# A planner that keeps engines apart on a PSUM bank and counts GpSimd and TensorE with other costs

## The chip, the cores and the metric

The kernel runs on one core of one Trainium2 chip. The metric is device time in microseconds, from several timed runs of the same program; the profile shows one execution of it, taken by the hardware profiler. TensorE (PE) multiplies and transposes, VectorE (DVE) and ScalarE (ACT) work on elements, GpSimd (POOL) takes some of DVE's work, and SyncE (SP) issues DMAs. PE alone writes PSUM here; DVE and ACT read it.

## The reference

Pooled attention for 4 batches of 8 heads, and then a low-rank mix over the tokens and an MLP, all in float32:

```python
q_pool = q.reshape(B, H, S // 2, 2, D).mean(axis=3)      # 4 x 8 x 576 x 64
scores = scale * np.matmul(q_pool, k.transpose(0, 1, 3, 2))   # S = 1152 keys
attn = np.exp(scores - max); attn = attn / (sum + 1e-9)
x = (attn @ v), heads joined                             # 4 x 576 x 512
u = x + ((x.T @ U) @ V).T                                # rank 32
out = u + np.maximum(u @ w_ch1, 0) @ w_ch2               # 512 -> 2048 -> 512
```

## The kernel before

**What is computed where.** Each of the 32 heads is one call of `head(n)`. The keys and queries of a head are turned by PE (L538 for queries, L616 for the keys of batches 0 and 1, L571 for those of batches 2 and 3), and the turned blocks are taken out of PSUM by ACT and DVE. In batches 2 and 3 this is `turn_whole`: ACT reads the bank in L580, L587, L591 and L595, DVE reads the same bank in L582. A scan finds row maxima: 14 products of 384 or 288 key columns on PE (L643, L645), each reduced by DVE (L649). Then 14 score products (L703 and L704, 256 to 640 columns in a bank) whose exponentials ACT writes to `big` (L710). DVE or POOL add up the exponentials into `acc` (L686). The values are 36 MATMUL instructions a head (L735), and the sums of a pair of heads are L726, L772, L759.

After the 8 heads of a batch comes `tail(b)`. First the low-rank mix: x times U (L818), a copy to SBUF by ACT (L824, L825), two DMAs that lay the copy beside itself (L827, issued by SP), an ACT copy (L828) and a DVE difference (L830), then that times V (L837) and five DVE additions into X (L839). Then X is turned (L909) and split by ACT and DVE (L918, L919). Then the MLP: 24 products for a block of the hidden layer (L943) or, in the last batch, a form with fewer products (L987), and the way back (L1058, L1062). The MLP of batch b runs among the heads of batch b+1. In the first batch the float64 weights are decoded (L415 to L427, L867, L868) by ACT, DVE and POOL.

**What sets the order.** No order is written by hand. Every piece of work is an `op` with a due number, the engines that can run it, a cost in nanoseconds for each, and the keys that it reads and writes. `Plan.run` is a greedy planner: it keeps a clock for each engine, and gives each the earliest-due op that can start at once or within 30 ns (`SLACK`) of the first. An op can start when its inputs are there (their planned end plus a latency from the table `LAT`), its engine is free and a buffer is free. Ops that DVE or POOL can run (`dual`: L514, L528, L686, L868, L962, L967) go to the one that would end first, with a bias of 300 ns for DVE; L551 goes to ACT or POOL. The planner's order is only the order in which each engine's instructions stand in the program. The waits are semaphores that the tile layer adds by itself. PSUM has 8 banks, 5 of them in pool `m` and 3 in pool `s`.

**Names that the change touches.** `Slot` is one buffer, a PSUM bank for `m` and `s`. `pick` chooses the next op of an engine; its last loop makes an op wait for the former users of a buffer (`b.wait`). `g_(n)` is the planned cost of n columns on POOL, `mm(n)` of n columns on PE, `TSW` what a group of value products costs beside its columns, `TP` and `TPR` what a transpose costs, `FILL` what one of the 70 filler transposes (L479) costs, which keep PE busy when it has nothing else to do early on.

Of the kernel before, what the change touches and what calls it, by code (L numbers as in the profile page):

```python
# [32 lines left out]

class Slot:
    def __init__(self, tile_):
        self.tile, self.user = tile_, None


class Op:
# [3 lines left out]
class Plan:  # L43
# [46 lines left out]
    def run(self, slack, bias, bias_from, link):  # L90

        lat = self.LAT
        for o in self.ops:
            o.open = len(o.deps)
            for d in o.deps:
                d.succ.append(o)
        free = dict.fromkeys(lat, 0.0)
        free["pool"] = 4000.0
        port = wire = 0.0
        cand = {e: [] for e in lat}  # L100
        key = lambda o: (o.at, o.seq)

        def offer(o):
            for e in o.ways:
                base = max([d.end + lat[d.way][e] for d in o.deps], default=0.0)
                cand[e].append((o.at, o.seq, base, o))
                cand[e].sort()

        def slot_of(b, e, taken=()):
            best = None  # L110
            if b.line and b.line[0] is not b:
                return None
            if b.keep and sum(s.user is None or not s.user.left for s in b.slots) <= b.keep:
                return None
            for s in b.slots:
                u = s.user
                if s in taken:
                    continue
                if u is None:
                    return 0.0, s  # L120
                if u.left == 0:
                    t = max(x.end + lat[x.way][e] for x in u.done)
                    if best is None or t < best[0]:
                        best = (t, s)
            return best

        def late(o, e, t):

            shift = bias if t > bias_from else 0.0
            for c in o.ways:  # L130
                if c != e:
                    end = free[c]
                    for at, seq, base, x in cand[c]:
                        if x is o:
                            if max(end, base) + o.ways[c][0] + (shift if c == "dve" else -shift) < t + o.ways[e][0]:
                                return True
                            break
                        if base <= end:
                            end += x.ways[c][0]
            return False  # L140

        def pick(e):

            found, first = [], None
            for at, seq, base, o in cand[e][:self.WINDOW]:
                t = max(base, free[e])
                if e == "pool" or (e == "dve" and o.port):
                    t = max(t, port)
                if e == "sp" and len(o.ways[e]) > 4:
                    t = max(t, wire - 1100)  # L150
                if first is not None and t > first + slack:
                    continue
                taken = []
                for b in o.bufs:
                    if b.slot is None:
                        got = slot_of(b, e, taken)
                        if got is None:
                            t = None
                            break
                        t = max(t, got[0])  # L160
                        taken.append(got[1])
                    else:
                        for x in b.wait:
                            t = max(t, x.end + lat[x.way][e])
                if t is None or (len(o.ways) > 1 and late(o, e, t)):
                    continue
                found.append((t, o))
                if first is None or t < first:
                    first = t
                if t <= free[e]:  # L170
                    break
            for t, o in found:
                if t <= first + slack:
                    return t, o
            return None

        for o in self.ops:
            if not o.open:
                offer(o)
        order, choice = [], dict.fromkeys(lat)  # L180
        while len(order) < len(self.ops):
            for e in lat:
                choice[e] = pick(e)
            e = min((c for c in lat if choice[c]), key=lambda c: choice[c][0])
            t, o = choice[e]
            for b in o.bufs:
                if b.slot is None:
                    b.slot = slot_of(b, e)[1]
                    if b.line:
                        b.line.popleft()  # L190
                    b.wait = b.slot.user.done if b.slot.user else ()
                    b.slot.user = b
                b.left -= 1
                b.done.append(o)
            cost = o.ways[e][0]
            o.way, o.start = e, t
            if e == "sp":
                hold, far = (*o.ways[e][2:], 0, 0, 0)[:2]
                issue = 475 + hold
                free[e] = t + issue + 25  # L200
                wire = max(wire, t + issue + 625) + cost
                o.end = wire + far
            else:
                free[e] = o.end = t + cost
                if len(o.ways[e]) > 2:
                    o.end += o.ways[e][2]
                if e == "pool" or (e == "dve" and o.port):
                    port = o.end
            for c in o.ways:
                cand[c] = [x for x in cand[c] if x[3] is not o]  # L210
            for x in o.succ:
                x.open -= 1
                if not x.open:
                    offer(x)
            order.append(o)
        self.order = order
        turn = None
        for o in order:
            ins = o.ways[o.way][1]()
            if o.way == "dve" and o.port:  # L220
                turn = ins
            elif o.way == "pool" and turn is not None:
                link(ins, turn)
                turn = None
# [3 lines left out]
def kernel(  # L228
# [25 lines left out]
    NJ = S // P  # L254
    HALF = NQ // 2
# [6 lines left out]
    QT, KS = -9.86, -11.64  # L262
# [2 lines left out]
    NB, QUICK = 320, (False, False, False, True)  # L265
    NARROW, NP2 = 256, 7
    GV = [((0, 6), (6, 9))] + [((0, 9),)] * 3
    TSW = 300.0
    SUM, AV, YT = 0.71, 0.51, 0.79
    NS = 6  # L270
    LOOSE = (1, 0, 0, 0)
    APART = (True, True, False, False)
    KT, MX0, MXS = 0.79, -8.77, 4.16
    V_LO = slice(2 * R, 3 * R)
    WARM_UP, WARM_N, FILL, FILL_N = 5000.0, 13, 90.0, 70
    NWHOLE = H + 1
    EXP_MIN, EXP_MAX = 2.0 ** -15, 122879.9921875
    SCALE = 0.5 / float(D) ** 0.5
# [13 lines left out]
    op = plan.op  # L292
    sb = ctx.enter_context(tc.tile_pool(name="sb", bufs=1))
    dram = ctx.enter_context(tc.tile_pool(name="dram", bufs=1, space=bass.MemoryType.DRAM))
    ps = ctx.enter_context(tc.tile_pool(name="ps", bufs=1, space=PSUM))

    def slots(name, n, shape, dtype=F32, pool=sb):
        return [Slot(pool.tile(shape, dtype, name=f"{name}{i}")) for i in range(n)]

    ident = sb.tile([P, P], F32, name="ident")  # L300
    identr = sb.tile([P, P], F32R, name="identr")
# [8 lines left out]
    def cut(of, first, n, shape, rows=P):  # L310
# [13 lines left out]
        qp=slots("qp", 1, [QP, NQT, D]),  # L324
        T1=cut(room, 0, 2, (S,)),
        T2=cut(room, 2 * S, 2, (S,), D + 1),
        Q1=cut(room, 5 * S, 2, (NQ,)),
        Q2=cut(room, 6 * S, 2, (PAD + NQ,), D + 1),
# [44 lines left out]
        return 0.52 * n + 67  # L373

    def g_(n):
        return 2.127 * n + 137

    def mm(n):
        return n / 2.4 + 13.0

    def copies(n, first, f, hold=0):

# [5 lines left out]
    def dual(n, f):  # L388
        return {"dve": (v_(n), lambda: f(nc.vector)), "pool": (g_(n), lambda: f(nc.gpsimd))}

    TP, TPR, MOVE = 109, 84, 130
    RATE, BULK = 330.0, True

    def dma(nbytes):
# [104 lines left out]
    def head(n):  # L499
        op = plan.op if n < len(heads) - 4 else lambda at, ways, r=(), w=(), port=False: plan.op(at, ways, [*r, *arena], w, port)  # L500
        b, h = heads[n]
        par = b % 2
        T = lambda G: begin(n) + G * (SLOT if n >= NWHOLE else SLOT * HEAD0 / HEAD)
# [33 lines left out]
                src = qp.t[:, 2 * t:2 * t + 2].rearrange("p a d -> p (a d)")  # L537
                nc.tensor.transpose(pt.t[:, t * QP:(t + 1) * QP], src, ident[0:QP, 0:QP])  # L538

        op(T(QT), ("pe", 240, qT), [qp, (Q1, "use"), (Q2, "use")], [pt])  # L540

        for e in range(2):
            rows, cs_ = slice(e * D, (e + 1) * D), slice(e * HALF, (e + 1) * HALF)
# [185 lines left out]
        for j0, j1 in GV[b]:  # L729
            last = j1 == NJ and odd and not APART[b]  # L730

            def value(js=range(j0, j1), last=last):
                for j in js:
                    for hf in range(2):
                        nc.tensor.matmul(pa.t[hf * D:(hf + 1) * D, 0:HALF], vt.t[:, j], pu[j].t[:, j % 2, hf * HALF:(hf + 1) * HALF],  # L735
                                         start=(j == 0), stop=(j == NJ - 1))
                if last:
                    total()

            n_ = j1 - j0 + last * parts  # L740
            op(T(j1 - 0.5 + AV), ("pe", n_ * 4 * (HALF / 2.4 + 2.0) + TSW, value),
               [(vt, 0)] + keys(range(j0, j1)) + (summed if last else []), [pa] + ([pk] if last else []))
        op(T(NJ + AV), ("act", a_(HALF, True), lambda: nc.scalar.activation(ay.t[:, odd], pa.t[:, 0:HALF], AF.Copy)), [pa], [(ay, odd)])

        if not odd:
            return
        if APART[b]:
            op(T(NJ + AV), ("pe", parts * 4 * (HALF / 2.4 + 2.0) + TSW, total), summed, [pk])
        op(T(NJ + AV), ("act", a_(HALF, True), lambda: nc.scalar.activation(sr.t, pk.t[:, 0:HALF], AF.Copy)), [pk], [sr])

        first = (0, P, HALF - P)
# [383 lines left out]
```

## Time and profile before

| | |
|---|---|
| median of 3 runs | 894.67 us (892.97 to 895.92) |
| span of the profiled execution | 891.4 us |
| granted TensorE clock | 1.000 of full speed |
| PE busy | 882.0 us |
| DVE busy | 742.6 us |
| ACT busy | 524.9 us |
| POOL busy | 220.3 us |

The profiled execution's span, from the first to the last instruction, is 3.3 us below the median of the timed runs, which hold some time around it. A busy share counts a MATMUL from its start to its modelled end. Two MATMULs overlap in the pipeline, so the next one can start some 0.15 us late, and the engine still counts as busy. Waits on PE are therefore read from the starts in the timeline: the distance from one start to the next.

### The profile page before, as it was taken

The numbers are of one execution on the slowest core, as the hardware profiler recorded it, in microseconds if no ns is written. First come the engines' busy times: TensorE is split into PE (matmuls) and PEld (weight loads), VectorE is DVE, ScalarE is ACT, GpSimd is POOL, SyncE is SP. The second block draws the span as 40 slices with busy tenths as digits, with TensorE's granted clock in tenths as the row PEclk, the third lists the DMA queues.
The fourth block names the chain that finished last, engine by engine and source line by source line (L and its number), as shares of the span: only waits on it lengthen the run. The fifth ranks groups of instructions, "written<-read, shape, count | busy, mean of one in ns | idle before, by whom it ended". The sixth has DMA issues, their size and how long they took to land.

```text
span 891.4 us, 15633 instructions
## 1 busy us (share of the span) xinstructions
PE 882.0 (99%) x5597; PEld 723.0 (81%) x5597; DVE 742.6 (83%) x1481; ACT 524.9 (59%) x1184; POOL 220.3 (25%) x223
## 2 busy tenths in 40 slices
PE   9999999999999999999999999999999999999998
PEld 8787777788787877798887887888878778899987
DVE  8999999889999899788888888787776564898885
ACT  6788888758787787565565657555663331322221
POOL 3334444344544635430001012200200000001110
PEclk9999999999999999999999999999999999999999
DMA  6244564346666564543242332422232255555422
GB/s 172 76 131 139 153 197 125 75 156 198 216 208 217 158 224 144 174 143 87 77 135 69 108 111 70 135 88 88 97 120 83 95 172 189 173 204 187 168 100 102
DMA packets 63635, 124.00 MB, mean 139 GB/s; under 512 B 5931, under 2 KB 33350, under 8 KB 63558
## 3 DMA queue, kind: packets, MB, share of 16 engines
q1 hardware_dynamic: 62214, 118.46, 41.0%
q10 hardware_dynamic: 1344, 4.56, 2.3%
q8 instruction: 44, 0.72, 0.4%
q14 instruction: 33, 0.27, 0.1%
HBM read 96.17 MB, written 21.50 MB: 132 GB/s over the span
## 4 chain that ended last, share of the span: by engine, by line
PE 61%; DVE 6%; ACT 1%; issue 1%; DMA 0%; DVEq 0%; ACTq 0%
PE m L1058 19%; PE m L943 11%; PE m L735 8%; PE s L987 6%; PE s L704 4%; PE s L703 4%; PE m L643 4%; DVE mp L649 1%; PE m L571 1%; DVE acc L686 1%; PE m L909 1%; PE m L759 1%; PE m L818 1%; PE m L726 1%; DVE w L868 0%
## 5 line engine op out<-in xcount | busy, mean ns | idle before, releaser
L710 ACT ACTIVATE big<-s 128x320 f32<-128x320 f32 (+2 forms) x448 | 204.2, 480 | 120.9 <-PE s L704 116.2
L649 DVE TENSOR_REDUCE mp<-m 128x1 f32<-128x384 f32 (+1 forms) x448 | 216.4, 532 | 21.9 <-PE m L643 20.4
L1058 PE MATMUL m<-w,hh 128*128 128x512 f32 x798 | 227.0, 397 | 0.0
L943 PE MATMUL m<-rest,w 128*128 128x512 f32 (+1 forms) x768 | 184.6, 354 | 0.0
L703 PE MATMUL s<-room 128*128 128x256 f32 (+2 forms) x576 | 169.1, 304 | 1.3 <-ACT big L710 0.9
L1058 PEld LDWEIGHTS m<-w,hh 128*128 128x128 f32 x798 | 144.2, 188 | 26.2 <-issue 3.1
L704 PE MATMUL s<-room 65*128 65x256 f32 (+2 forms) x576 | 165.1, 298 | 0.0
L735 PE MATMUL m<-big,v 128*64 128x288 f32 x1152 | 148.5, 410 | 0.0
L943 PEld LDWEIGHTS m<-rest,w 128*128 128x128 f32 x768 | 132.4, 188 | 15.3 <-issue 2.2
L686 POOL TENSOR_TENSOR acc<-acc,big 128x576 f32<-128x576 f32 x66 | 94.2, 1427 | 150.2 <-ACT big L710 68.6
L686 DVE TENSOR_TENSOR acc<-acc,big 128x576 f32<-128x576 f32 x150 | 120.4, 803 | 13.1 <-ACT big L710 10.2
L643 PE MATMUL m<-room 128*128 128x384 f32 x384 | 128.4, 358 | 0.5 <-DVE mp L649 0.3
L735 PEld LDWEIGHTS m<-big,v 128*64 128x64 f32 x1152 | 79.2, 137 | 55.5 <-issue 2.0
L703 PEld LDWEIGHTS s<-room 128*128 128x128 f32 x576 | 109.0, 189 | 13.9 <-issue 4.4
L704 PEld LDWEIGHTS s<-room 65*128 65x128 f32 x576 | 108.9, 189 | 6.0 <-DMA room<-mr 0.2
L643 PEld LDWEIGHTS m<-room 128*128 128x128 f32 x384 | 69.6, 189 | 17.6 <-DVE mp L649 3.1
L383 ACT ACTIVATE room<-m 64x288 fp32r<-64x288 f32 (+1 forms) x173 | 72.3, 427 | 9.0 <-PE m L538 6.4
L1062 DVE TENSOR_TENSOR X<-m,X 128x512 f32<-128x512 f32 x95 | 64.7, 683 | 11.0 <-PE m L1058 10.6
L427 POOL TENSOR_TENSOR wt<-wt,rx 128x512 int32<-128x512 int32 (+2 forms) x35 | 44.4, 1269 | 80.8 <-DVE wt L425 19.1
L551 POOL CAST qb<-room 64x64 fp32r<-64x64 f32 x56 | 15.8, 283 | 171.8 <-DVE acc L686 114.2
L947 ACT ACTIVATE hh<-m 128x512 fp32r<-128x512 f32 (+1 forms) x64 | 33.0, 515 | 32.3 <-PE m L943 29.6
L949 DVE SCALAR_TENSOR_TENSOR hh<-m,hh 128x512 fp32r<-128x512 f32 (+1 forms) x64 | 37.4, 584 | 16.2 <-ACT hh L947 15.9
(134 smaller groups left out, 1064.7 us busy)
## 6 DMA issues: line engine op xcount, KB each, us to landing
w<-wc SPq DMA_DIRECT2D x96, 512.0 KB
rx<-in_moe_w_ch_dram SPq DMA_DIRECT2D x32, 512.0 KB
wc<-w SPq DMA_DIRECT2D x32, 512.0 KB
q<-in_q_dram SPq DMA_DIRECT2D x32, 288.0 KB
v<-in_v_dram SPq DMA_DIRECT2D x32, 288.0 KB
k<-in_k_dram SPq DMA_DIRECT2D x31, 288.0 KB
room<-room ACTq DMA_DIRECT2D x15, 288.0 KB
out_dram<-X SPq DMA_DIRECT2D x11, 256.0 KB
```

What stands on the lines that cost most here:

```text
L383: ways = {"act": (a_(n, True) + hold, lambda: f(lambda o, i: nc.scalar.activation(o, i, AF.Copy)))}
L643: nc.tensor.matmul(pm.t[:, 0:w], Q1.t[:, t * P - 64:t * P + 64], T1.t[:, cs_], start=True, stop=True)
L649: op(T(MX0 + 0.3 + MXS * u / 14), ("dve", v_(w), lambda c=c, t=t, w=w, pm=pm: nc.vector.reduce_max(mp.t[:, c * 5 + t:c * 5 + t + 1], pm.t[ ...
L686: op(at, dual(NQ, lambda e: e.tensor_tensor(acc.t, a(), b_(), op=ALU.add)), r, [acc])
L703: nc.tensor.matmul(o, T1.t[:, kc], Q1.t[:, qa:qz], start=True, stop=False)
L704: nc.tensor.matmul(o, T2.t[:, kc], Q2.t[:, PAD + qa:PAD + qz], start=False, stop=True)
L710: op(T(when + 0.1), ("act", a_(len(js) * nq, True), lambda js=js, qa=qa, qz=qz, nq=nq, ss=ss, p=pu[j], e=js[0] % 2: nc.scalar.activation(p ...
L735: nc.tensor.matmul(pa.t[hf * D:(hf + 1) * D, 0:HALF], vt.t[:, j], pu[j].t[:, j % 2, hf * HALF:(hf + 1) * HALF], start=(j == 0), stop=(j == ...
L943: op(now, ("pe", mm(nb), lambda c=c, i=i, a=a, bb=bb, w=w, ph=ph, sl=sl: nc.tensor.matmul(ph.t[:, 0:nb], w.t[:, a, c * P:(c + 1) * P], (ul ...
L987: nc.tensor.matmul(bank.t[:, 0:NB], left(a, c), ub.t[:, i, bb, c], start=(c == 0 and j == 0), stop=(c == 1 and j == 2))
L1058: op(now, ("pe", mm(512), lambda f=f, i=i, a=a, bb=bb, w=w, h_=h_: nc.tensor.matmul(po.t, h_.t[:, a, ns], w.t[:, bb], start=(f == fg and i ...
L1062: op(now, ("dve", v_(512), lambda: nc.vector.tensor_tensor(x(), po.t, x(), op=ALU.add)), [po], bk[t])
```

## The change

Each PSUM slot gets a table `seen`: for each engine the last op planned on the bank, by whichever buffer held it. In `pick`, an op on a bank is planned no sooner than the last op of every other engine on this bank has ended, plus the latency from `LAT`. Before, two engines that read one bank could be planned at the same time. The loops of the kernel, the arithmetic and the number of buffers stay as they are, and so do `LAT`, `BIAS`, the due numbers and the choice between engines.

The costs that change: a POOL op by 140 ns more; a PE product of n columns 0.4427 n + 5.5 ns for n / 2.4 + 13 (512 columns 232 for 226, 256 columns 119 for 120); 9 blocks of values 4,521 ns for 4,692; the sums of a pair of heads get 130 ns instead of `TSW`; transposes 89 and 86 ns for 109 and 84; a filler 82 for 90.

```diff
 class Slot:
     def __init__(self, tile_):
-        self.tile, self.user = tile_, None
+        self.tile, self.user, self.seen = tile_, None, None
...
                     else:
                         for x in b.wait:
                             t = max(t, x.end + lat[x.way][e])
+                        for c, x in (b.slot.seen or {}).items():
+                            if c != e:
+                                t = max(t, x.end + lat[c][e])
...
+            for b in o.bufs:
+                if b.slot.seen is not None:
+                    b.slot.seen[e] = o
...
-    TSW = 300.0
+    TSW, TOT = 165.0, 130.0
...
-    WARM_UP, WARM_N, FILL, FILL_N = 5000.0, 13, 90.0, 70
+    WARM_UP, WARM_N, FILL, FILL_N = 5000.0, 13, 82.0, 70
...
     def g_(n):
-        return 2.127 * n + 137
+        return 2.127 * n + 277
     def mm(n):
-        return n / 2.4 + 13.0
+        return 0.4427 * n + 5.5
...
-    TP, TPR, MOVE = 109, 84, 130
+    TP, TPR, MOVE = 89, 86, 130
...
-            op(T(j1 - 0.5 + AV), ("pe", n_ * 4 * (HALF / 2.4 + 2.0) + TSW, value),
+            op(T(j1 - 0.5 + AV), ("pe", n_ * 4 * (HALF / 2.4 + 1.0) + TSW + last * TOT, value),
```

The instructions of PE are the same 4,943 in both programs, in another order. The order changes on all engines, nearly from the start. POOL has 219 for 228 instructions that belong to the work: 6 fewer L514, 4 fewer L551, 2 fewer L686, 1 fewer L868, and 2 more L528, 1 more L962, 1 more L967. What POOL gives up, DVE has, and in the case of L551 ACT. The lines of the changed kernel are numbered 9 higher from L475 on, so that L837 is L846 there.

The first place is PE behind the low-rank mix of batch 0. L837 (L846 after) adds the mix, L909 (L918) turns X for the MLP, L703 and L704 (L712 and L713) are scores of the next head; `m_` and `s_` are PSUM banks. Before:

```order
L837 MATMUL m_120<-xs_111,Vst 128x512
L837 MATMUL m_121<-xs_111,Vst 128x512
L837 MATMUL m_123<-xs_111,Vst 128x512
L837 MATMUL m_119<-xs_111,Vst 128x512
L837 MATMUL m_122<-xs_111,Vst 64x512
L703 MATMUL s_118<-room 128x320
L704 MATMUL s_118<-room 128x320
L909 MATMUL m_120<-ident,X_98 128x128 x4
L909 MATMUL m_121<-ident,X_98 128x128 x4
L703 MATMUL s_117<-room 128x320
L704 MATMUL s_117<-room 128x320
L909 MATMUL m_123<-ident,X_98 128x128 x4
```

On PE at the same place in the changed program:

```order
L846 MATMUL m_123<-xs_111,Vst 128x512
L712 MATMUL s_118<-room 128x288
L713 MATMUL s_118<-room 128x288
L846 MATMUL m_119<-xs_111,Vst 128x512
L846 MATMUL m_122<-xs_111,Vst 128x512
L846 MATMUL m_123<-xs_111,Vst 128x512
L846 MATMUL m_119<-xs_111,Vst 64x512
L918 MATMUL m_122<-ident,X_98 128x128 x4
L918 MATMUL m_123<-ident,X_98 128x128 x4
L918 MATMUL m_119<-ident,X_98 128x128 x4
L918 MATMUL m_122<-ident,X_98 128x128 x4
L735 MATMUL m_123<-acc_82,ones 32x288
```

The scores that stood between the turns of X now stand ahead of the mix, and the mix goes round three banks for five.

The second place is ACT at the start of batch 2, where a head's keys are taken out of one bank (`m_122` before, `m_119` after) into `room` by L580, L591 and L587 (L589, L600 and L596 after). DVE reads the same bank in L582 (L591 after, on DVE). Before:

```order
L580 ACTIVATE room<-m_122 64x4x128
L867 ACTIVATE w_2_109<-wt_102 128x512
L580 ACTIVATE room<-m_122 64x4x128
L591 ACTIVATE room<-m_122 128x512
L710 ACTIVATE big<-s_116 128x320
L419 ACTIVATE wt_103<-rx 128x512
L420 ACTIVATE rx<-rx 128x512
L587 ACTIVATE room<-m_122 64x4x128 x2
```

On ACT at the same place in the changed program:

```order
L589 ACTIVATE room<-m_119 64x4x128 x2
L600 ACTIVATE room<-m_119 128x512
L562 ACTIVATE qb_80<-room 64x64
L596 ACTIVATE room<-m_119 64x4x128 x2
L428 ACTIVATE wt_102<-rx 128x512
L429 ACTIVATE rx<-rx 128x512
L822 ACTIVATE xs_111<-X_99 128x512
```

ACT's five reads of the bank now stand close together, and on DVE other work has come between the two reads of this bank, which stood side by side.

## Rows read from the trace of the kernel before

**Rows 1.** The page: span, and busy time of each engine.
```profile
span 891.4 us, 15633 instructions
PE 882.0 (99%) x5597; PEld 723.0 (81%) x5597; DVE 742.6 (83%) x1481; ACT 524.9 (59%) x1184; POOL 220.3 (25%) x223
```
**Rows 2.** Busy time by stretch: PE, PEld, DVE, ACT, POOL (instructions), clock, DMA.
```profile
0.00:180.00 180.00, 175.08 (x1300) 137.99 (x1300) 166.98 (x360) 146.21 (x336) 71.99 (x83) 1.00 0.47 133
180.00:360.00 180.00, 179.17 (x1091) 142.55 (x1090) 170.25 (x332) 136.01 (x296) 85.07 (x69) 1.00 0.59 194
```
**Rows 3.** PE's timeline: start, length, instruction [idle before <-releaser].
```profile
155.25 0.34 PE L643 MATMUL m<-room 128*128 128x384 f32 x1
155.43 0.31 PE L703 MATMUL s<-room 128*128 128x320 f32 x1
...
155.72 0.34 PE L643 MATMUL m<-room 128*128 128x384 f32 x1
156.27 0.39 PE L703 MATMUL s<-room 128*128 128x256 f32 x1 [0.21 <-ACT big L710]
```
**Rows 4.** Waits of PE's weight loads, 20 to 180 us: total us, times, longest.
```profile
PEld s L703 <- ACT big L710: 3.4, 9, 0.6
PEld m L643 <- ACT big L710: 1.9, 4, 0.5
PEld m L643 <- DVE mp L649: 1.1, 3, 0.6
```
**Rows 5.** Waits over the whole span: who waited for whom.
```profile
DVE room L582 <- ACT room L591: 11.8, 15, 1.3
ACT room L587 <- DVE room L582: 9.5, 13, 0.8
```
**Rows 6.** Waits of PE's weight loads, 360 to 720 us.
```profile
PEld m L759 <- ACT room L587: 0.5, 2, 0.2
```
**Rows 7.** Groups by line on POOL and DVE: busy us, mean ns, idle before.
```profile
L686 POOL TENSOR_TENSOR acc<-acc,big 128x576 f32<-128x576 f32 x66 | 94.2, 1427 | 150.2 <-ACT big L710 68.6 <-DVE mp L649 38.8 <-DVE acc L686 24.5
L514 DVE TENSOR_TENSOR qp<-q 96x384 f32<-96x384 f32 x15 | 8.7, 580 | 1.7 <-DMA q<-in_q_dram 1.6
L686 DVE TENSOR_TENSOR acc<-acc,big 128x576 f32<-128x576 f32 x150 | 120.4, 803 | 13.1 <-ACT big L710 10.2 <-DVE acc L686 0.5
```
**Rows 8.** PE's part of the chain that ended last: start us, us, what.
```profile
740.02 5.51 PE m L943 x24
```
**Rows 9.** Timelines of PE and DVE at the low-rank mix of batch 0.
```profile
161.93 0.45 PE L818 MATMUL m<-xs,U 128*64 128x512 f32 x1
...
169.56 1.43 PE L837 MATMUL m<-xs,Vst 128*128 128x512 f32 x5 [1.18 <-DVE xs L830]
170.82 0.31 PE L703 MATMUL s<-room 128*128 128x320 f32 x1
...
171.12 1.04 PE L909 MATMUL m<-ident,X 128*128 128x128 f32 x8
171.91 0.40 PE L703 MATMUL s<-room 128*128 128x320 f32 x1
...
175.79 6.43 PE L943 MATMUL m<-rest,w 128*128 128x512 f32 x27
...
170.12 2.48 DVE L839 TENSOR_TENSOR X<-m,X 128x512 f32<-128x512 f32 x4
...
173.12 2.47 DVE L919 TENSOR_TENSOR rest<-m,rest 128x512 fp32r<-128x512 f32 x4
```
**Rows 10.** PE's timeline at the mix of batch 1 and of batch 3.
```profile
358.23 0.39 PE L818 MATMUL m<-xs,U 128*64 128x512 f32 x1
...
365.39 1.43 PE L837 MATMUL m<-xs,Vst 128*128 128x512 f32 x5
...
724.60 0.39 PE L818 MATMUL m<-xs,U 128*64 128x512 f32 x1
...
731.07 0.50 PE L837 MATMUL m<-xs,Vst 128*128 128x512 f32 x1 [0.32 <-DVE xs L830]
```

More of the change, by code (lines that the diff above doesn't have):

```diff
@@ L297, in slots @@
     def slots(name, n, shape, dtype=F32, pool=sb):
-        return [Slot(pool.tile(shape, dtype, name=f"{name}{i}")) for i in range(n)]
+        made = [Slot(pool.tile(shape, dtype, name=f"{name}{i}")) for i in range(n)]
+        for x in made if pool is ps else ():
+            x.seen = {}
+        return made
     ident = sb.tile([P, P], F32, name="ident")
@@ L538, in qT @@
                 nc.tensor.transpose(pt.t[:, t * QP:(t + 1) * QP], src, ident[0:QP, 0:QP])
-        op(T(QT), ("pe", 240, qT), [qp, (Q1, "use"), (Q2, "use")], [pt])
+        op(T(QT), ("pe", 194, qT), [qp, (Q1, "use"), (Q2, "use")], [pt])
         for e in range(2):
@@ L747, in head @@
         if APART[b]:
-            op(T(NJ + AV), ("pe", parts * 4 * (HALF / 2.4 + 2.0) + TSW, total), summed, [pk])
+            op(T(NJ + AV), ("pe", parts * 4 * (HALF / 2.4 + 1.0) + TOT, total), summed, [pk])
         op(T(NJ + AV), ("act", a_(HALF, True), lambda: nc.scalar.activation(sr.t, pk.t[:, 0:HALF], AF.Copy)), [pk], [sr])
```

## The prediction

> **What bounds the kernel now.** I read the page first. PE is busy for 882.0 of a span of 891.4 us [rows 1], so the time is PE's work and whatever PE waits. The change adds and removes no PE instruction. It can only change the waits.
>
> Next came the table by stretch [rows 2]. In the first 360 us DVE is busy for 166.98 and 170.25 us of 180 each, that is 93 and 95 per cent, and POOL for less than half. PE shows 4.9 us of idle time in the first stretch, 0.8 in the second. So DVE is the second bound of the first two batches, and that is where PE waits.
>
> Then the timeline of PE, because its busy share hides waits [rows 3]. L643 at 155.25 is followed by the next start 0.18 us later. The same instruction at 155.72 is followed by one at 156.27, 0.55 us later: PE waited 0.37 us, of which the row shows 0.21, for the exponentials of L710. Waits of this kind are many and small. Between 20 and 180 us PE's weight loads waited 3.4 and 1.9 us for L710 and 1.1 us for the maxima of L649 [rows 4], 6.4 us together.
>
> I read the low-rank mix last, since it is a chain that PE must sit out if it has nothing else to do: L818, two copies on ACT, two DMAs, ACT, DVE, L837. From the start of the last L818 to the start of L837 it took 7.63 us in batch 0 (161.93 to 169.56) [rows 9], 7.16 us in batch 1 and 6.47 us in batch 3 [rows 10].
>
> **The change part by part.** All sums are made against the span of 891.4 us; the median of the timed runs is 3.3 us above it.
>
> *PE's own work:* nothing. The instructions are the same, and a planned cost is not a duration.
>
> *The bank rule.* In batches 2 and 3 ACT and DVE take turns on the turned keys. DVE's L582 sat idle 11.8 us for ACT's L591 and ACT's L587 9.5 us for L582 [rows 5], some 0.75 us each time. So the program already holds the two apart, and the old planner did not know it. The new order puts ACT's reads together and other work between DVE's, which takes much of this idle time away. But it is idle time of ACT and DVE. Of PE's waits in these batches only 0.5 us is put down to L587 [rows 6], because DVE has room there and PE has other heads' work. I count a gain between nothing and 2.5 us, which is five times that row, for what comes late behind it without being named; I take 1.0, nearer to the row.
>
> ACT L587's 9.5 us are 13 waits of 0.73 us on a bank of which the two engines read different halves of the partitions, for the first L587 and the second L582 at least [rows 5]. The Trainium skill (PSUM — Partial Sum Buffer, "PSUM bank collisions raise a hardware error") asks for a guard by bank and 32-partition quadrant only, and calls the whole bank the simple version; by that, the planner now keeps apart what might overlap. If the two did overlap, the new rule would give away up to these 9.5 us of ACT's time, and PE nothing like it. The row says that the program waits in either case, so by the row the rule costs nothing, and I go by the row.
>
> *The costs of POOL.* An addition of 576 columns on POOL took 1,427 ns [rows 7]; the old plan said 1,362, the new one says 1,502. The old value was 65 ns too low and the new one is 75 too high, while the bias of 300 ns for DVE stays. So the planner gives POOL less: 9 instructions less on the whole, among them 6 L514 and 2 L686. On DVE these cost 6 x 0.58 + 2 x 0.80 us = 5.1 us [rows 7], less 2 L528 that go the other way at about the 0.80 us of L686, which has the same 576 columns: 3.5 us more on DVE. If DVE's idle time covers it, it costs nothing; if all of it falls where DVE is the bound it costs 3.5 us. DVE was idle for 22.8 us of the first 360 [rows 2], so most is covered, and I take 0.5.
>
> *The mix of batch 0.* Before, between L837 and the first L943 PE was at work nearly all the time, for 6.23 us (169.56 to 175.79) [rows 9]. DVE was busy without a break there: L839 from 170.12, L919 until 175.59. L943 comes 0.2 us after DVE's end, so DVE sets this distance, and the change leaves DVE's nine instructions as they are. In the new order fewer instructions stand here: five L837 (1.26 us, 169.56 to 170.82), 16 turns L909 (0.79 us for 8, so 1.58), one score pair (0.29), L726, one L645 and three turns, an estimated 1.0 us by the columns. That is 4.1 us of work in 6.2 us. PE waits about 2.1 us; before it waited some 0.4. This costs 1.7 us.
>
> Ahead of L837 stand 33 rows of the order from the last L818 on in the new program: 8 L643 at 0.18, six score pairs of 320 columns at 0.29 [rows 3], two groups of two pairs of 256 columns at 0.48 and a pair of 288 at 0.27 by the same rows and their columns, six turns at 0.10 (0.79 us for 8 [rows 9]), and L818 itself at 0.23, as any product of 512 columns (5.51 us for 24 [rows 8]). That is 5.3 us. With a chain between 6.47 and 7.63 us PE waits 1.2 to 2.3 us; before it waited 1.18 by the row, about 1.4 by the starts. I take 1.8, so 0.4 more. Together the mix of batch 0 costs 2.1 us (1.5 to 2.6).
>
> *The mix of batch 1.* Here the new order has from the last L818 to the first L837 14 products of 512 columns at 0.23 [rows 8], some 0.7 us of turns, 0.48 us of scores and L818: 4.6 us for a chain of 6.47 to 7.16 us. PE waits 1.9 to 2.6 us. Before, 32 rows stood there, and with them the 7.16 us held about 0.5 us of waits [rows 10]. This costs 1.4 to 2.1 us; I take 1.6. Why the planner leaves the gap: work that was due earlier has been done ahead of the chain, and the next head waits for ACT and DVE.
>
> *The many small waits before 180 us.* The 6.4 us of [rows 4] may shrink, since the plan now knows POOL's lateness and the PE clock better. They may also grow, since products of 512 columns are no longer planned too short, which had hidden some slack. Their place is where DVE is at 93 per cent, and a better order does not make DVE faster. I take a gain of 1.5 us, bounds from 4.0 gained, which is some two thirds of the row, to 1.5 lost.
>
> The sum: -1.0 + 0.5 + 2.1 + 1.6 - 1.5 = +1.7 us, so a span of 893.1 and a median of 896.4 us. With all bounds at their good ends: -2.5 + 0 + 1.5 + 1.4 - 4.0 = -3.6, a median of 891.1. With all at their bad ends: 0 + 3.5 + 2.6 + 2.1 + 1.5 = +9.7, a median of 904.4.
>
> **The rivals.**
>
> *Slower, by DVE in the first two batches.* The 3.5 us that move from POOL to DVE lie in full on the path, because 93 to 95 per cent busy [rows 2] is as full as a queue gets whose work must come in order; L649 then frees the scan's banks late and PE waits for it. With the two mixes (3.7 us) and no gain in the small waits this is +7.2 us, 901.9. For it: [rows 2, 4]. Against it: L514 can be done long before it is needed. It decides from the point where DVE's waits in the first 360 us fall well below 22.8 us in sum.
>
> *Faster, by a plan that holds.* If the planned starts on ACT, DVE and POOL come true, the small waits of [rows 4] go for the most part (5 us), the turns on one bank bring their 2.5 us, and the work done ahead of the mixes is a gain elsewhere that pays for half of their 3.7 us. That is -5.6 us, a median of 889.0. For it: each term of the plan that was wrong is now nearer. Against it: the waits lie where an engine is full, not where the plan is wrong, and where the plan was most wrong (the turns on one bank) PE hardly waits.
>
> *It does nothing that reaches PE.* The waits of ACT and DVE on a bank fall, and PE's total stays within a microsecond: 894.7. This is part of "no change".
>
> **How the numbers follow.** About 0.3 per cent, 2.7 us, is what a measurement of this kernel can tell from no change. The forecast with its own spread, together with the rival that nothing reaches PE, has 0.40 within this bound. Slower has 0.34: the DVE rival 0.2, the bad ends of the forecast 0.14. Faster has 0.26: the planned one 0.18, the good ends 0.08. The forecast is 896.4 us. The range goes from 888 to 904: below it lies about one in ten, from the faster rival, and above it about one in ten, from the slower one with its bounds at their bad ends.
>
> **What would show it.** In the profile of the changed kernel the sum of the waits between L582 and L587 or L591 (L591, L596, L600 there) should fall to less than half, with PE's waits in batches 2 and 3 as before. At the mix of batch 0 the first L943 (L952) should come about 6.2 us behind the first L837 (L846), with about 2 us of PE idle between them. At the mix of batch 1 L846 should start 1.9 to 2.6 us late. DVE should be above 93 and 95 per cent in the first two stretches. The forecast is wrong if DVE's idle time there does not move or grows while PE waits less for L710 and L649, or if the chains of the mix are shorter than 6.4 us.

## The result and the profile after

The changed kernel is slower: 903.08 us median (901.34 to 903.76, 4 runs) for 893.82 us (the three runs of the kernel before and a fourth of 892.45), a ratio of 1.0099 (95% interval 1.0079 to 1.0119), or 9.3 us. The span of the profiled execution is 899.5 us, 8.1 us more than before. The page of the changed kernel, span and busy time of each engine:

```profile
span 899.5 us, 15650 instructions
PE 886.4 (99%) x5597; PEld 722.8 (80%) x5597; DVE 738.2 (82%) x1486; ACT 525.3 (58%) x1188; POOL 213.6 (24%) x214
```

Set beside [rows 1], PE has the same 5,597 instructions, and no engine has more than 0.4 us more work apart from PE, whose busy time includes hidden waits. So the 8.1 us should be waits of PE. They can be counted. For each MATMUL I took the distance from its start to the next start, less the usual distance for its line and columns, and summed what exceeds 25 ns, without the switches in and out of the narrow products (L735, L726). This gives 34.4 us before and 42.6 us after. The difference of 8.2 us is the difference of the spans. By stretches of 90 us the growth is 3.1 us (90 to 180), 3.8 (180 to 270) and 1.6 (360 to 450), and between 1.0 us less and 0.8 more in each of the others.

The table by stretch of the changed kernel, which answers to [rows 2] (PE, PEld, DVE, ACT, POOL, clock, DMA):

```profile
0.00:180.00 180.00, 173.59 (x1282) 136.75 (x1282) 167.67 (x359) 146.63 (x340) 68.11 (x78) 1.00 0.47 134
180.00:360.00 180.00, 178.38 (x1073) 138.45 (x1072) 164.77 (x328) 132.41 (x289) 72.78 (x60) 1.00 0.56 186
```

DVE did not become fuller: in the first 360 us it is busy for 332.4 us, where it was 337.2, with 0.7 us more in the first stretch and 5.5 less in the second. Part of this is that the changed kernel has come less far by 360 us. But over the whole execution, too, DVE has five instructions more and 4.4 us less work. Its largest group, L686 of [rows 7] (L695 here), took 772 ns on the mean for 803; why, no run shows:

```profile
L695 DVE TENSOR_TENSOR acc<-acc,big 128x576 f32<-128x576 f32 x154 | 118.8, 772 | 9.5 <-ACT big L719 6.9 <-ACT mr L683 0.5
```

The largest single piece is the mix of batch 0. PE's timeline there, in the changed kernel (L827 is L818 of before, L846 is L837, L918 is L909, L952 is L943):

```profile
169.45 0.39 PE L827 MATMUL m<-xs,U 128*64 128x512 f32 x1
...
175.22 0.28 PE L713 MATMUL s<-room 65*128 65x256 f32 x1
178.05 0.41 PE L712 MATMUL s<-room 128*128 128x320 f32 x1 [2.55 <-ACT big L719]
...
179.22 0.40 PE L846 MATMUL m<-xs,Vst 128*128 128x512 f32 x1
...
179.73 1.73 PE L846 MATMUL m<-xs,Vst 128*128 128x512 f32 x4
181.60 1.84 PE L918 MATMUL m<-ident,X 128*128 128x128 f32 x12
183.67 0.65 PE L918 MATMUL m<-ident,X 128*128 128x128 f32 x4 [0.23 <-DVE rest L928]
...
186.13 1.19 PE L952 MATMUL m<-rest,w 128*128 128x512 f32 x4
```

From the last L827 to the first L952 it takes 16.68 us, where it took 13.86 (161.93 to 175.79 [rows 9]), and PE does less work in it. By the starts PE waits 6.9 us here; before it was 1.9. The long wait of 2.55 us is for L719, the exponentials. ACT's timeline shows why they were late, and the row of DVE below it when the chain's last step ran:

```profile
176.48 0.63 ACT L837 ACTIVATE xs<-tr 128x512 fp32r<-128x512 f32 x1 [1.79 <-DMA tr<-tr]
177.02 0.66 ACT L429 ACTIVATE rx<-rx 128x512 int32<-128x512 uint32 x1
177.56 2.78 ACT L719 ACTIVATE big<-s 128x320 f32<-128x320 f32 x7
...
177.15 0.68 DVE L839 TENSOR_TENSOR xs<-tr,xs 32x512 fp32r<-32x512 f32 x1 [1.13 <-ACT xs L837]
```

ACT sat 1.79 us at the copy of the mix (L837 here, L828 before) until the DMAs had landed, then did a step of the decoding (L429, L420 before), and behind both stood seven exponentials in the queue, which PE needed for its score banks. SP issued the two DMAs in 1.79 us:

```profile
171.10 1.79 SPq L836 DMA_DIRECT2D tr<-tr  x2
```

The rest of the growth is spread. Counted by the same pieces of work instead of by the clock, PE's waits fell by about 0.6 us up to this mix, grew by 5.0 in it, by about 2 in many small waits of the heads behind it (186.13 to 370.81 us), and by about 1.2 from the last L827 to the first L952 of batch 1. From there to the end they are about 10 us in both kernels.

### The profile page after: what moved, and what is told of

It is laid out like the page before. It is cut to its first block, busy times and chain, and to the rows that moved or that the text cites. A ratio compares the mean times of both kernels' runs of the same rounds, so it can differ in the third digit from the quotient of the medians.

```text
span 899.5 us, 15650 instructions
## 1 busy us (share of the span) xinstructions
PE 886.4 (99%) x5597; PEld 722.8 (80%) x5597; DVE 738.2 (82%) x1486; ACT 525.3 (58%) x1188; POOL 213.6 (24%) x214
## 4 chain that ended last, share of the span: by engine, by line
PE 69%; DVE 4%; ACT 1%; issue 1%; DMA 0%; ACTq 0%; DVEq 0%
PE m L1067 20%; PE m L952 14%; PE m L744 10%; PE s L996 5%; PE s L712 5%; PE s L713 5%; PE m L652 4%; DVE mp L658 1%; PE m L580 1%; PE m L735 1%; PE m L768 1%; PE m L918 1%; DVE acc L695 1%; PE m L654 1%; PE m L827 1%
## 5 line engine op out<-in xcount | busy, mean ns | idle before, releaser
L719 ACT ACTIVATE big<-s 128x320 f32<-128x320 f32 (+2 forms) x448 | 201.3, 479 | 103.8 <-PE s L713 98.5
L1067 PE MATMUL m<-w,hh 128*128 128x512 f32 x798 | 222.1, 397 | 0.3 <-DVE hh L958 0.3
L952 PE MATMUL m<-rest,w 128*128 128x512 f32 (+1 forms) x768 | 184.5, 356 | 0.5 <-DVE rest L928 0.3
L712 PE MATMUL s<-room 128*128 128x256 f32 (+2 forms) x576 | 168.6, 304 | 3.2 <-ACT big L719 2.9
L713 PE MATMUL s<-room 65*128 65x256 f32 (+2 forms) x576 | 164.6, 297 | 0.6 <-DMA room<-mr 0.6
L952 PEld LDWEIGHTS m<-rest,w 128*128 128x128 f32 x768 | 132.2, 188 | 18.5 <-issue 3.1
L695 POOL TENSOR_TENSOR acc<-acc,big 128x576 f32<-128x576 f32 x62 | 88.4, 1425 | 194.2 <-DVE acc L695 83.0
L652 PE MATMUL m<-room 128*128 128x384 f32 x384 | 126.0, 356 | 0.8 <-DVE mp L658 0.5
L695 DVE TENSOR_TENSOR acc<-acc,big 128x576 f32<-128x576 f32 x154 | 118.8, 772 | 9.5 <-ACT big L719 6.9
L712 PEld LDWEIGHTS s<-room 128*128 128x128 f32 x576 | 109.0, 189 | 15.1 <-ACT big L719 6.1
L713 PEld LDWEIGHTS s<-room 65*128 65x128 f32 x576 | 109.0, 189 | 5.6 <-issue 0.8
L652 PEld LDWEIGHTS m<-room 128*128 128x128 f32 x384 | 69.2, 189 | 17.2 <-DVE mp L658 6.0
L436 POOL TENSOR_TENSOR wt<-wt,rx 128x512 int32<-128x512 int32 (+2 forms) x35 | 44.8, 1279 | 78.1 <-DVE wt L434 18.9
L591 DVE TENSOR_TENSOR room<-m,room 64x512 fp32r<-64x512 f32 (+1 forms) x48 | 26.6, 554 | 30.3 <-ACT room L596 28.9
```

The source lines that it names most:

```text
L652: nc.tensor.matmul(pm.t[:, 0:w], Q1.t[:, t * P - 64:t * P + 64], T1.t[:, cs_], start=True, stop=True)
L695: op(at, dual(NQ, lambda e: e.tensor_tensor(acc.t, a(), b_(), op=ALU.add)), r, [acc])
L712: nc.tensor.matmul(o, T1.t[:, kc], Q1.t[:, qa:qz], start=True, stop=False)
L713: nc.tensor.matmul(o, T2.t[:, kc], Q2.t[:, PAD + qa:PAD + qz], start=False, stop=True)
L719: op(T(when + 0.1), ("act", a_(len(js) * nq, True), lambda js=js, qa=qa, qz=qz, nq=nq, ss=ss, p=pu[j], e=js[0] % 2: nc.scalar.activation(p ...
L952: op(now, ("pe", mm(nb), lambda c=c, i=i, a=a, bb=bb, w=w, ph=ph, sl=sl: nc.tensor.matmul(ph.t[:, 0:nb], w.t[:, a, c * P:(c + 1) * P], (ul ...
```

## The experiments

Four theories run through them. A: the new costs make the loss. B: the bank rule makes it. C: the old order was a picked one, since the due numbers had been picked for the old costs, and another order of the same planner loses whichever number is moved. D: the rule and the costs themselves make a worse order. The planner also tells when it thinks PE's work ends. This planned end is no time on the chip; it is in the table to show what the planner knows of its own order. The ratio is to the kernel before as it was run beside each (893.4 to 893.8 us); the first row gives one of these medians. The fifth column is the sum of PE's waits by the starts, in the profiled execution, the last one the part of it at the mix of batch 0.

| kernel | median us | ratio to before (95%) | planned end of PE | PE waits us | at the mix |
|---|---|---|---|---|---|
| before | 893.5 | | 867.7 | 34.4 | 1.9 |
| changed | 903.1 | 1.0099 (1.0079 to 1.0119) | 878.9 | 42.6 | 6.9 |
| e1_bank | 899.6 | 1.0069 (1.0052 to 1.0085) | 872.3 | 37.7 | 1.9 |
| e2_costs | 904.2 | 1.0113 (1.0095 to 1.0130) | 878.2 | 45.6 | 7.4 |
| e3_pool | 904.0 | 1.0113 (1.0096 to 1.0130) | 879.6 | 44.8 | 6.2 |
| e4_pe | 905.7 | 1.0129 (1.0111 to 1.0147) | 873.5 | 45.0 | 3.8 |
| n1_pool_1ns | 900.5 | 1.0081 (1.0065 to 1.0098) | 875.5 | 43.9 | 3.7 |
| n2_turn_1ns | 893.8 | 1.0008 (0.9995 to 1.0020) | 868.3 | 35.6 | 1.9 |
| n3_after_move_up | 901.8 | 1.0091 (1.0076 to 1.0106) | 876.6 | 43.3 | 6.9 |
| n4_after_move_down | 900.6 | 1.0075 (1.0060 to 1.0090) | 877.9 | 41.4 | 4.2 |
| r1_due | 892.6 | 0.9989 (0.9980 to 0.9998) | 867.2 | 34.6 | 0.4 |
| r2_due | 891.9 | 0.9984 (0.9974 to 0.9993) | 868.7 | 33.5 | 1.6 |
| r3_due_late | 892.8 | 0.9997 (0.9987 to 1.0007) | 868.0 | 35.8 | 2.3 |
| late_after | 902.2 | 1.0094 (1.0080 to 1.0108) | 879.7 | 41.8 | 5.8 |

The fifth column holds more than waits where TensorE's granted clock fell to 1.2 GHz for a stretch of the profiled execution, since at that clock the starts of products that do not wait lie further apart, too. Counted in the same way, this is some 1.7 us in e2_costs, 1.5 in e3_pool, 3.0 in n1_pool_1ns, 4.5 in n3_after_move_up, 1.5 in r1_due and 2.6 in r3_due_late. In e2_costs, e3_pool and n3_after_move_up 1.7, 1.5 and 3.0 us of this stand at the mix.

The fourth column can be had without the chip, and it holds most of the loss already: 11.2 us for the whole change, where 9.3 were measured, 7.8 for n1_pool_1ns (7.0), 0.6 for n2_turn_1ns (0.3).

### One part at a time

e1_bank, the kernel before with `seen` alone:

```diff
...
+                        for c, x in (b.slot.seen or {}).items():
+                            if c != e:
+                                t = max(t, x.end + lat[c][e])
...
```

> The bank rule alone, with all old costs. Theory A (the costs of PE and POOL make the loss): within 2.7 us of the kernel before, 891 to 897 us, and the waits of ACT and DVE for each other on the bank of the turned keys fall by half or more. Theory B (the bank rule makes the loss): 900 to 905 us. Theory C (any order that is far from the old one loses, whichever part makes it): slower by 4 to 10 us, 898 to 904 us, with the loss in places that have nothing to do with shared banks, the mix of batch 0 among them.

e2_costs, the changed kernel without these lines, with all its costs:

> All new costs, without the bank rule. Theory A: 900 to 905 us, as the whole change. Theory B: within 2.7 us of the kernel before. Theory C: slower by 4 to 10 us, and the loss of this run and of the bank rule alone do not add up to the 9.3 us of the whole change.

e3_pool, the kernel before with one new cost:

```diff
-        return 2.127 * n + 137
+        return 2.127 * n + 277
```

> Only the 140 ns more for each GpSimd operation. The rival of the prediction (work goes from GpSimd to VectorE, which is the bound of the first 360 us): slower by 3 to 7 us with VectorE busier in the first 360 us than before (337.2 us). If the move is covered: within 2.7 us. Theory C: slower by 4 to 10 us without VectorE being busier.

e4_pe, the kernel before with all the new PE costs and nothing else, among them:

```diff
-    TSW = 300.0
+    TSW, TOT = 165.0, 130.0
...
-        return n / 2.4 + 13.0
+        return 0.4427 * n + 5.5
...
-    TP, TPR, MOVE = 109, 84, 130
+    TP, TPR, MOVE = 89, 86, 130
...
```

> Only the new TensorE costs (products, value groups, sums, transposes, filler). If costs nearer to the trace make a better plan: faster by 2 to 6 us. If the slack that the old costs left for products of 512 columns was of use: slower by 2 to 5 us, spread over the small waits. Theory C: slower by 4 to 10 us.

Each part alone loses: 6.2, 10.8, 10.6 and 12.3 us against 893.4. They do not add up. The cost of POOL and the costs of PE lose 22.9 us one by one and 10.8 together, and with the bank rule on top the loss is 9.3. Theories A and B each fall, because each expected one part to be harmless. One caution on A: e1_bank's execution at full clock took 896.6 us, which is within what A allowed, and the three with a mean clock of 0.998 took 899.0 to 900.5; so about half of its 6.2 us is seen only in executions with the lower clock. That every part loses and that the losses do not add up is as theory C expected, but it had them too small (4 to 10 us) and had named the mix of batch 0 as one of the places in e1_bank, which is wrong (see below). For e4_pe none of the expectations reached as far as 12.3 us.

The prediction's rival, DVE as the bound, falls with e3_pool, as far as DVE's busy time tells. The table by stretch of e3_pool has

```profile
0.00:180.00 180.00, 174.97 (x1291) 137.83 (x1292) 168.89 (x362) 147.64 (x340) 61.99 (x73) 0.99 0.46 134
180.00:360.00 180.00, 178.07 (x1068) 139.21 (x1067) 166.27 (x332) 130.76 (x280) 71.88 (x62) 1.00 0.54 181
```

so DVE is busy for 335.2 us of the first 360, where it was 337.2, while POOL has 133.9 us for 157.1, and the kernel is 10.6 us slower. (Over the whole execution DVE has 751.0 us for 742.6 there, so work did move to it.) e1_bank does what the rule says. Its only wait above 1.5 us in sum between DVE and ACT on the bank of the turned keys is

```profile
DVE room L591 <- ACT room L596: 26.0, 12, 2.5
```

where before both sides waited [rows 5]. The kernel leaves the mix of batch 0 alone (1.9 us of waits, as before) and loses elsewhere.

### One nanosecond

n1_pool_1ns and n2_turn_1ns, the kernel before with one number moved:

```diff
-        return 2.127 * n + 137
+        return 2.127 * n + 138
```

> The kernel before with one planned cost moved by 1 ns: a GpSimd operation 2.127 n + 138 for 137. The order of every engine changes (on TensorE 4,428 lines of difference), the costs mean the same. Theory C (the old order is a picked one, and any other order of the same planner loses): slower by 4 to 12 us, 898 to 906 us. Theory D (a plan with nearly the same costs is as good as the old one, and the loss of the change comes from its costs and rule): within 2.7 us, 891 to 897 us.

```diff
-    TP, TPR, MOVE = 109, 84, 130
+    TP, TPR, MOVE = 110, 84, 130
```

> The kernel before with the planned cost of a transpose at 110 ns for 109, which changes 2,725 lines of TensorE's order. Theory C: slower by 4 to 12 us, less if the part of the order that stays holds the places that count. Theory D: within 2.7 us.

n3_after_move_up and n4_after_move_down, the changed kernel with `MOVE` at 131 and at 129 for 130:

> The changed kernel with one planned cost moved by 1 ns: a copy that moves partitions 131 for 130. Theory C: anywhere from 896 to 908 us, away from the 903.1 us of the changed kernel by more than its scatter of 2.4 us is as likely as not. Theory D: 901 to 905 us, as the changed kernel.

> The changed kernel with the same planned cost at 129 for 130. Theory C: 896 to 908 us, and other than the run with 131. Theory D: 901 to 905 us.

A nanosecond on POOL costs 7.0 us. It has no meaning as a cost; it only makes the greedy planner fall into another order, with 3.7 us of waits at the mix and most of the others elsewhere. A nanosecond on transposes costs nothing: 2,725 lines of PE's order change, but the mix of batch 0 stays as it was, and so do the waits in sum. This was theory C's own reserve, and it is also what theory D expected. The two neighbours of the changed kernel are 1.3 and 2.5 us below it, but their intervals overlap its own, so they do not tell C from D. What is shown here is that a move away from the old order can by itself lose most of what the whole change loses; n2_turn_1ns shows that not every move does.

### Due numbers picked anew

The due numbers decide which op goes first. The old ones look picked: with the old costs, a search over 20 of them that only asks the planner for its planned end of PE, without the chip, gained 0.3 us in 1,139 tries. With the new rule and costs the same search gained 10 us in as many. r1_due, r2_due and r3_due_late are the changed kernel with such numbers, the rule and the costs of PE and POOL untouched. Among the 20 are two that are not due numbers, the planner's patience `SLACK` and DVE's `BIAS`; what these two do alone was not run. Some of r1_due's:

```diff
-    HEAD0, HEAD = 16.77e3, 21.01e3
+    HEAD0, HEAD = 16723.2631, 21002.118
-    DEC_START, DEC_LEAD = 99.4e3, 12.6e3
+    DEC_START, DEC_LEAD = 97103.3182, 11948.362
-    SLACK = 30.0
+    SLACK = 18.1322
-    BIAS, BIAS_FROM = -300.0, 0.0
+    BIAS, BIAS_FROM = -337.0879, 0.0
```

> The changed kernel with its due numbers picked anew (when a head's steps are due, the heads' distance, the start of the decoding, the planner's patience, VectorE's bias), picked by the planner's own planned end of TensorE's work, which they bring from 878.9 back to 867.2 us; before the change it is 867.7. Rule and costs are those of the change. Theory C (due numbers had been picked for the old costs, and any shift of costs throws the picked order away): the loss goes, 889 to 895 us, and the mix of batch 0 holds about 2 us of TensorE waits for 6.9 in the changed kernel. Theory D (the new rule and costs themselves make a worse order): 900 us or more.

> As the run before, another pick, with a planned end of 868.7 us. Theory C: 890 to 897 us, a little above the first pick. Theory D: 900 us or more.

r3_due_late has numbers of its own and this cost besides, as has late_after, which keeps the old due numbers:

```diff
-... nc.sync.dma_start(tr()[c * R:(c + 1) * R], tr()[0:R]), 175), ...
+... nc.sync.dma_start(tr()[c * R:(c + 1) * R], tr()[0:R]), 175, 1500), ...
```

> A third pick, planned end 868.0 us, for the changed kernel with one more cost: the two DMAs of the mix (L836) are planned to land 1.5 us later, as the traces show them to. If ScalarE's early wait for them costs what it seems to at the mix: 887 to 892 us, below the first pick. If other work waits instead: 890 to 896 us.

> The changed kernel with its old due numbers, and the two DMAs of the mix planned to land 1.5 us later. In the changed kernel ScalarE waited 1.79 us for them with seven exponentials queued behind, and TensorE 2.7 us for those. If that wait is the cause of the mix's loss: TensorE's waits at the mix of batch 0 fall from 6.9 to about 4 us and the time to 899 to 901 us. If the mix is slow since the plan has no work for TensorE there: the waits move to other instructions and the time stays at 902 to 905 us.

All three picks are back where the kernel before was, by their ratios 9 to 10 us below the changed kernel, and two are a little below the old one: r2_due by 0.16 per cent (0.07 to 0.26). At the mix r1_due has 0.4 us of waits, less than the 2 expected. Theory D falls: nothing in the rule or the costs keeps the planner from an order as good as the old one. Whether a new pick for the old costs would have come out lower still was not run. PE's timeline at the mix of batch 0 in r2_due:

```profile
161.54 0.39 PE L827 MATMUL m<-xs,U 128*64 128x512 f32 x1
...
170.43 1.44 PE L846 MATMUL m<-xs,Vst 128*128 128x512 f32 x5
...
177.44 2.92 PE L952 MATMUL m<-rest,w 128*128 128x512 f32 x12
```

From L827 to L952 it takes 15.9 us, not much less than in the changed kernel, but with 1.6 us of waits instead of 6.9: PE has other heads' work in between. The chain of the mix is not shorter; it is filled.

late_after tells what ACT's early wait was worth. With the DMAs planned to land later, ACT waits 0.45 us for 1.79, and some of the exponentials stand ahead of the copy:

```profile
174.78 0.68 ACT L429 ACTIVATE rx<-rx 128x512 int32<-128x512 uint32 x1
175.35 0.42 ACT L719 ACTIVATE big<-s 128x320 f32<-128x320 f32 x1
176.22 0.63 ACT L837 ACTIVATE xs<-tr 128x512 fp32r<-128x512 f32 x1 [0.45 <-DMA tr<-tr]
```

PE's wait for them goes from 2.55 us to 0.17. But PE's waits at the mix only fall from 6.9 to 5.8 us. The time of 902.2 us is within the second expectation, and its interval overlaps that of the changed kernel. PE now waits for DVE's X, rest and other ends of the chain:

```profile
175.82 0.42 PE L712 MATMUL s<-room 128*128 128x320 f32 x1 [0.17 <-ACT big L719]
180.11 1.04 PE L846 MATMUL m<-xs,Vst 128*128 128x512 f32 x2 [0.39 <-DVE X L848]
183.53 0.65 PE L918 MATMUL m<-ident,X 128*128 128x128 f32 x4 [0.39 <-DVE rest L928]
184.82 0.44 PE L547 MATMUL m<-ident,qp 96*128 96x96 f32 x3 [0.46 <-DVE rest L928]
```

A cost nearer to the trace again bought nothing that can be told from no change as long as the due numbers stayed. r3_due_late, which has both, is no better than the picks without it, and so within its second expectation.

## Why the prediction was right in part

*What bounds the kernel* held. PE's work is fixed, the change moved its waits, and the waits by the starts account for the whole difference.

*The forecast* of 896.4 us, "no change" as the likeliest case, was too low by 6.7 us; 903.1 lies near the upper end of the range, 904, and in the case "slower" with its 0.34. That it lies inside is in part luck: the upper end was put together with 3.5 us for DVE on the path. The rival "slower, by DVE" came to 901.9 us and is nearly right in time, but its mechanism is wrong: DVE was less busy in the first 360 us (332.4 us for 337.2), so its idle time there grew from 22.8 to 27.6 us, where the rival needed it to fall well below 22.8. e3_pool shows the same with 24.8. That the move from POOL to DVE was covered, as the term of 0.5 us had it, agrees with this; no run shows it alone.

*The mix of batch 0* was the right place with the wrong size: 2.1 us more waits were expected, 5.0 came. Behind L846 the step held: 6.91 us from the first L846 (179.22) to L952 (186.13) with about 2.5 us of PE waits, for 6.2 and 2.1 predicted. Ahead of it the chain was mis-sized: 1.8 us of waits were expected, some 4.4 came. I took 6.47 to 7.63 us from three batches of the old trace; it took 9.77 (169.45 to 179.22). Of these, 8.4 us ran until DVE's L839 had ended (177.83), for 7.6 before (161.93 to 169.50). The rows of before (L827, L828 and L830 there are L836, L837 and L839 in the changed kernel) show where the difference lies:

```profile
163.62 1.23 SPq L827 DMA_DIRECT2D tr<-tr  x2
...
168.16 0.63 ACT L828 ACTIVATE xs<-tr 128x512 fp32r<-128x512 f32 x1 [1.92 <-DMA tr<-tr]
...
168.82 0.68 DVE L830 TENSOR_TENSOR xs<-tr,xs 32x512 fp32r<-32x512 f32 x1 [2.55 <-ACT xs L828]
```

From the issue of the two DMAs to ACT's copy 4.5 us passed before and 5.4 in the changed kernel (171.10 to 176.48); why, no run shows. PE's work ahead of L846 was counted nearly right: nine L652 (L643 before) stand there for the eight of the sum. In the last 1.4 us of the 9.77 L846 stood behind score products that waited for the exponentials, and these stood behind ACT's wait for the DMA. I had costed PE's missing work, and not asked what stands behind a wait in ACT's queue. But late_after, with this wait nearly gone, still takes 9.34 us ahead of L846, so the queue is the smaller part.

*The mix of batch 1* was expected to cost 1.6 us. PE's timeline there in the changed kernel:

```profile
370.81 0.40 PE L827 MATMUL m<-xs,U 128*64 128x512 f32 x1
...
374.53 1.65 PE L1067 MATMUL m<-w,hh 128*128 128x512 f32 x6 [0.32 <-DVE hh L958]
377.26 0.50 PE L846 MATMUL m<-xs,Vst 128*128 128x512 f32 x1 [0.61 <-DVE xs L839]
...
397.59 0.47 PE L547 MATMUL m<-ident,qp 96*128 96x96 f32 x3 [0.20 <-DVE rest L928]
398.33 1.73 PE L952 MATMUL m<-rest,w 128*128 128x320 f32 x10 [0.27 <-DVE rest L928]
```

The chain took 6.45 us, at the short end of the range I gave, and held 1.4 us of waits for 0.5 before; L846 started some 0.8 us late, not the 1.9 to 2.6 expected. 1.1 us more came later, where the turns of X were late for L952 (L943 before), but this stretch had waits before too. From the last L827 to the first L952 the growth is about 1.2 us, near the 1.6 expected.

*The bank rule* was expected to gain 1.0 us and gained nothing. ACT's waits for DVE on the bank are gone, but DVE waits longer at a time (waits over the whole span of the changed kernel):

```profile
DVE room L591 <- ACT room L596: 28.9, 12, 2.5
ACT room L596 <- DVE room L591: 0.2, 1, 0.2
```

The sum of both directions fell from 41.7 us to 29.7 over all of the bank's lines, and only from 30.5 to 29.4 for those that I had named, not to less than half as I had written. PE's waits from the first L943 of batch 1 (L952) on are about 10 us in both kernels, as I had written. The rule gave no gain, since it is about waits that PE did not feel [rows 6].

*The small waits before 180 us* were expected to fall by 1.5 us. They fell by less. The three rows of [rows 4], which had 6.4 us, have 8.6, but 2.8 of these are the one wait at the mix, which is counted there. The other 5.8 us are 0.6 less than before (waits of PE's weight loads, 20 to 180 us, in the changed kernel):

```profile
PEld s L712 <- ACT big L719: 5.5, 11, 2.8
...
PEld m L652 <- DVE mp L658: 2.2, 8, 0.4
...
PEld m L652 <- ACT big L719: 0.9, 2, 0.5
```

*What failed in the sum:* the term that was most mis-sized is the mix of batch 0, 5.0 us for 2.1, mostly ahead of L846. Gains of 2.5 us were counted for the bank rule and the small waits, and some 0.6 came. And no term held the 2 us in the heads behind the mix. Behind these stands a question that I did not ask. I asked what each rule and cost is worth, and not whether the due numbers still fit; n1_pool_1ns loses 7.0 us with no rule and no real cost, and the three picks take the loss back with rule and costs kept. The planner's own planned end, 867.7 us for the old kernel and 878.9 for the changed one, would have told of a loss of this size before any run.

What stays open is why e4_pe, whose planned end of 873.5 us is among the better ones, is the slowest on the chip. The planned end sorts the other kernels roughly; it does not explain this one. Open too is what in the old order keeps n2_turn_1ns from losing.

## What to carry to other kernels

A list of due numbers that was picked by trial can be fitted to the planner's costs; change a cost, even to a truer one, and pick the numbers again before judging the cost. Compare the planner's planned end before and after the change, since it costs no run. To tell a bad rule from a lost pick, move some meaningless numbers by their smallest step and see how far the time goes: here one step of 1 ns cost 7.0 us, three quarters of what the whole change cost, and another nothing. And at a chain that an engine must sit out, look at what stands behind each waiting instruction in every queue, not only at how much work is left for the engine that ends last.

## What the hardware showed that was not expected

In some of the profiled executions TensorE's granted clock fell to half, 1.2 GHz, between 134 and 180 us, after PE had waited. In the profile of n1_pool_1ns PE waited 1.75 us for the small DMA that lays the row of maxima; this is PE's timeline, and below it the table by stretch (PE, PEld, DVE, ACT, POOL, clock, DMA, GB/s):

```profile
146.69 0.35 PE L703 MATMUL s<-room 128*128 128x256 f32 x1
148.80 0.58 PE L704 MATMUL s<-room 65*128 65x256 f32 x1 [1.75 <-DMA room<-mr]
...
150.59 5.67 PE L735 MATMUL m<-big,v 128*64 128x288 f32 x26
```
```profile
144.00:148.40 4.40, 2.96 (x21) 2.23 (x20) 4.40 (x11) 4.34 (x13) 0.04 (x1) 1.00 0.30 120
148.40:155.30 6.90, 6.50 (x25) 3.42 (x27) 5.92 (x11) 5.65 (x12) 2.17 (x2) 0.51 0.44 121
```

In the 4.4 us before, PE was busy for 2.96 us; in the 6.9 us behind, the clock column reads 0.51. The first 26 value products took 5.67 us. In the kernel before, 36 of the same shape took 4.59 us at 2.4 GHz:

```profile
372.87 4.59 PE L735 MATMUL m<-big,v 128*64 128x288 f32 x36
```

Such a fall is not in every execution of a kernel. The changed kernel's profiled execution had none and was its fastest with 901.34 us; the other three have a mean clock of 0.998 and took 902.7 to 903.8 us, so about 1.7 us of the loss of 9.3 go with the clock. By the starts, the one stretch at 1.2 GHz cost 1.7 us in e2_costs and 1.5 in e3_pool. All executions of the kernel before have 0.999 or 1.000. That PE's waits bring the fall about is not shown: the profiled executions with a fall have waits of 1.1 to 2.4 us shortly ahead of it, but the wait of 2.55 us in the changed kernel was followed by none, and no run changed the waits alone.
